# The first load of an attention block, issued as two halves of 64 rows from two engines

## The chip, the cores and the metric

The kernel runs on one core of a Trainium2 chip. A core has TensorE (PE, matmuls), VectorE (DVE), ScalarE (ACT), GpSimd (POOL) and SyncE (SP), and 16 DMA engines that carry the transfers. SyncE and ScalarE can each issue transfers, each into a queue of its own; on chip memory has 128 rows (partitions). The metric is the time of one execution in microseconds (us). Before the change the median of three runs is 1300.84 us (1300.77 to 1301.26).

## The reference

One decoding step of a transformer block, two tokens in the batch, 32 heads, 8192 cached keys and values for each, all in 32 bit floats:

```python
B, Sq, D = 2, 1, 512
H, Sk, Dh = 32, 8192, 128
q = (x @ wq).reshape(B, Sq, H, Dh)          # x is layer-normalised first
scores = einsum("bhqd,bhkd->bhqk", q, k_cache) * (Dh ** -0.5)
p = softmax(scores)
o = einsum("bhqk,bhkd->bhqd", p, v_cache)
h = x + o @ wo
out = h + relu(layernorm(h) @ w1 + b1) ** 2 @ w2 + b2   # F = 1792
```

Keys and values are 64 pairs (batch, head) of 8 MB each, 512 MB in all; the weights wq and wo are 8 MB each.

## The kernel before

On-chip memory holds a ring of three places, each 128 rows of 64 KB (`ring`, `place(u)`). The host has laid out the keys and values of each pair as such a block of 128 rows (`kvd[i]`, keys in the first half of each row, values in the second) and the query weights in the same form (`wqd`), so that each load is one transfer of 128 rows.

Start: place 2 is loaded with the query weights (line 213), issued by SyncE, then x is loaded twice into two rows of `xr` (line 216, after a memset of `xr` on VectorE), then the first two pairs go into places 0 and 1 (line 218). VectorE and ScalarE normalise x, TensorE turns it (`xn`) and multiplies it with the query weights in place 2 (64 matmuls), turns the result, and VectorE writes the queries `QT`, `q3` and `QR`. Once the query matmuls are done, SyncE issues the load of pair 2 into place 2 (line 307).

Loop: 21 rounds of three pairs. For each pair TensorE makes the scores (line 345), VectorE their negated maximum (351), ScalarE the exponentials (358), VectorE the four sums weighted with the values (363) and a copy of the statistics (367), which frees the place. SyncE waits for that and issues the next load into the place (329). The last pair, `wo`, `w1` and `w2` follow by the same queue in pieces, and the feed-forward part runs at the end.

What sets the order: the program is written out by hand. Outside the loop it goes through the class `Line`. `Line.load(out, in_, engine="sp")` records one transfer that the named engine issues (line 136), with a semaphore of its own; `plan` works out from the regions which earlier operations each one waits for, and lets SyncE have at most `AHEAD` = 8 of these loads under way. Loads issued by another engine are not counted there. Operations keep their order on each engine. The operations that read all of place 2 wait for every load that wrote to it.

Of the kernel before, what the change touches and what calls it, by code (L numbers as in the profile page):

```python
# [10 lines left out]
P = 128  # L11
# [162 lines left out]
def attention_block_kernel(nc, xd, kvd, wqd, wod, w1d, w2d, out):  # L174
    def sb(name, *shape):
        return nc.alloc_sbuf_tensor(name, [P, *shape], F32).ap()

    written = nc.alloc_semaphore("written")
    line = Line(nc)
    pe, dve, act, sp = nc.tensor, nc.vector, nc.scalar, nc.sync  # L180
# [11 lines left out]
    def place(u):  # L192
        return ring[:, u * ROW : (u + 1) * ROW]
# [16 lines left out]


    xr = sb("xr", D)
    line.load(place(2), wqd)
    line.memset(xr, 0.0)
    for at in (0, 32):
        line.load(xr[at : at + B], xd)
# [406 lines left out]
```

## Time and profile before

| | us |
|---|---|
| median of three runs | 1300.84 |
| the profiled execution | 1301.16 |
| its span | 1299.8 |
| VectorE busy | 742.9 |
| TensorE busy | 422.4 |
| ScalarE busy | 143.7 |

The profile is of one execution. A line of the timeline gives start and duration in us, the engine and the line of the program, the operation, what it writes and reads, and in brackets how long the engine was idle before it and what ended that. "SPq" is the issue of a transfer by SyncE. "DMA" in a page is the busy share of the 16 DMA engines in tenths in each of 40 equal slices of the span, "GB/s" what they moved in each. A row of DMA issues ends with the median us from the issue to the landing. In a row by stretches the last two columns are the DMA share and the rate.

### The profile page before, as it was taken

Reading aid. Unit: us, or ns where it says so; the run is one execution under the profiler, and the core shown is the slowest. Engines: PE = TensorE matmul, PEld = TensorE weight load, DVE = VectorE, ACT = ScalarE, POOL = GpSimd, SP = SyncE. Lnnn points to the kernel's source line nnn. Section 1 sums busy time; section 2 is a strip of 40 time slices with the busy share of each in tenths; the row PEclk is TensorE's granted clock in tenths of the full one; section 3 lists DMA queues with packets and bytes.
Section 4 is the critical chain, followed back from the end, with each engine's and each line's share of the span. In section 5 each row is a group of like instructions: output and inputs, shape, how many; then the busy total and the mean of one; then the engine's idle time right before and its main releaser. Section 6 shows DMA issues by size and latency. Waiting matters only on the chain. (4 is left out here: it accounts for less than half of the span.)

```text
span 1299.8 us, 6711 instructions
## 1 busy us (share of the span) xinstructions
PE 422.4 (32%) x2418; PEld 113.7 (9%) x2418; DVE 742.9 (57%) x709; ACT 143.7 (11%) x149; POOL 0.7 (0%) x6
## 2 busy tenths in 40 slices
PE   1423233223323323313313323322323332331347
PEld 0100000000000000000000000000000000000012
DVE  1355655655665564665665565665566565657474
ACT  1110010111011011011011011011101011101111
POOL 0000000000000000000000000000000000000000
PEclk9766566666566566656566556656656656666678
DMA  9999999999999999999999999999999999999998
GB/s 420 420 450 419 450 421 442 430 426 446 422 448 421 450 422 442 430 430 442 422 450 421 448 424 448 422 450 421 436 436 421 450 422 448 424 448 422 450 412 371
DMA packets 11069, 561.16 MB, mean 432 GB/s; under 512 B 1234, under 2 KB 1332, under 8 KB 1720
## 3 DMA queue, kind: packets, MB, share of 16 engines
q1 hardware_dynamic: 11064, 561.08, 99.7%
q8 instruction: 4, 0.07, 0.0%
q14 instruction: 1, 0.01, 0.0%
HBM read 561.03 MB, written 0.05 MB: 432 GB/s over the span
## 5 line engine op out<-in xcount | busy, mean ns | idle before, releaser
L345 PE MATMUL s<-ring,q 128*32 128x512 f32 x2016 | 376.1, 914 | 831.2 <-PEq L318 831.2
L363 DVE SCALAR_TENSOR_TENSOR ring<-ring,s 128x2048 f32<-128x2048 f32 x252 | 561.5, 2285 | 143.1 <-DVEq L318 143.1
L351 DVE TENSOR_REDUCE st<-s 128x1 f32<-128x2048 f32 x63 | 144.4, 2292 | 341.9 <-DVEq L318 341.9
L358 ACT ACTIVATE s<-s,st 128x2048 f32<-128x2048 f32 x63 | 122.3, 1942 | 1083.4 <-ACTq L318 1083.4
L345 PEld LDWEIGHTS s<-ring,q 128*32 128x32 f32 x2016 | 94.5, 159 | 1112.0 <-issue 1112.0
L363 DVE DVE_READ_ACCUMULATOR ring<-ring,s 128x1 f32 x252 | 21.0, 83 | 0.0
L367 DVE TENSOR_SCALAR ALL<-st 128x6 f32 x63 | 10.8, 172 | 15.2 <-DVEq L318 15.2
L165 DVE TENSOR_REDUCE sx<-xr 2x1 f32<-2x512 f32 x1 | 0.7, 676 | 21.2 <-DMA xr<-in_xd 21.2
L358 ACT ACTIVATION_READ_ACCUMULATOR s<-s,st 128x1 f32 x63 | 12.1, 193 | 0.0
L139 PE MATMUL s<-ring,OT 128*2 128x512 f32 (+1 forms) x70 | 10.8, 689 | 3.6 <-DMA ring<-in_wod 3.0
L139 PE MATMUL s<-ident,xr 128*128 128x4 f32 x8 | 1.9, 356 | 26.0 <-DVE xr L157 26.0
L139 PE MATMUL s<-ring,xn 128*2 128x512 f32 x64 | 9.2, 742 | 0.3 <-DVE xn L150 0.3
L161 DVE SCALAR_TENSOR_TENSOR ring<-ring,s 128x2048 f32<-128x2048 f32 x3 | 6.8, 2283 | 1.4 <-DMA ring<-in_kvd 1.4
L139 PE MATMUL s<-ring,QR 128*32 128x512 f32 x32 | 5.3, 825 | 4.6 <-DMA ring<-in_kvd 4.6
L157 DVE TENSOR_SCALAR QT<-s 128x64 f32<-128x64 f32 x1 | 0.2, 225 | 10.3 <-PE s L139 10.3
L139 PE MATMUL s<-ring,xc 128*2 128x448 f32 (+1 forms) x34 | 5.6, 725 | 0.3 <-DVE xc L153 0.3
L143 ACT ACT_TABLE_LOAD x4 | 5.1, 1283 | 0.8 <-PEq L615 0.7
L354 DVE TENSOR_SCALAR q<-QT 128x96 f32 x21 | 5.1, 243 | 0.0
L139 PE MATMUL s<-ALL,pick 128*128 128x62 f32 (+1 forms) x16 | 3.4, 352 | 5.1 <-PEq L464 4.5
L139 PE MATMUL s<-ring,a 128*2 128x128 f32 x112 | 3.6, 272 | 2.5 <-DMA ring<-in_w2d 1.8
L139 PEld LDWEIGHTS s<-ident,xr 128*128 128x128 f32 x8 | 1.8, 327 | 26.0 <-DVE xr L157 26.0
L150 DVE COPY res<-s 128x128 f32<-128x128 f32 x1 | 0.3, 292 | 5.9 <-PE s L139 5.9
(86 smaller groups left out, 50.9 us busy)
## 6 DMA issues: line engine op xcount, KB each, us to landing
ring<-in_kvd SPq DMA_DIRECT2D x1, 4096.0 KB, 28.3
ring<-in_wod SPq DMA_DIRECT2D x1, 4096.0 KB, 18.1
ring<-in_kvd SPq DMA_DIRECT2D x1, 3584.0 KB, 26.3
ring<-in_w1d SPq DMA_DIRECT2D x2, 1792.0 KB, 24.8
ring<-in_wod SPq DMA_DIRECT2D x1, 2560.0 KB, 31.8
ring<-in_w2d SPq DMA_DIRECT2D x2, 1280.0 KB, 30.5
ring<-in_wod SPq DMA_DIRECT2D x1, 1568.0 KB, 18.2
ring<-in_kvd SPq DMA_DIRECT2D x63, 37.3
```

The lines of the kernel that those rows point to most:

```text
L139: self.op("pe", lambda e: e.matmul(out, lhsT, rhs, start=start, stop=stop), [lhsT, rhs], [out])
L143: self.op("act", lambda e: e.activation(out, in_, func, bias=bias, scale=scale, accum_out=accum_out), [in_, *more], [out] + ([] if accum_o ...
L150: self.op("dve", lambda e: e.tensor_copy(out, in_), [in_], [out])
L157: self.op("dve", lambda e: e.tensor_scalar(out, in_, by, None, op0=ALU.mult), [in_, *more], [out])
L161: self.op("dve", lambda e: e.scalar_tensor_tensor(out, a, by, b, op0=op0, op1=op1, accum_out=accum_out), [a, b, *more], [out] + ([] if acc ...
L165: self.op("dve", lambda e: e.tensor_reduce(out, in_, axis=AX.X, op=op, negate=negate), [in_], [out])
L345: made = pe.matmul(bk[n][32 * j : 32 * j + 32, :], q3[:, u, :], keys(u)[:, j, n * BLK : (n + 1) * BLK], start=True, stop=True)
L351: dve.tensor_reduce(nm, s, axis=AX.X, op=ALU.max, negate=True).then_inc(m_full, 1)
L354: dve.tensor_scalar(q3, nxt[:, :, None].to_broadcast([P, SLOTS, 32]), 1.0, None, op0=ALU.mult)
L358: act.activation(s, s, AF.Exp, bias=nm, scale=1.0, accum_out=ls).then_inc(e_full, 1)
L363: made = dve.scalar_tensor_tensor(v, v, 1.0, s, op0=ALU.mult, op1=ALU.mult, accum_out=st3[:, u, 2 + e : 3 + e])
L367: dve.tensor_scalar(all3[:, bass.ds(r, 1), u], st3[:, u : u + 1], 1.0, None, op0=ALU.mult).then_inc(kv_free, 1)
```

## The change

The load of the query weights into place 2 is issued as two loads of 64 rows. Rows 0 to 63 stay with SyncE, as its first issue. Rows 64 to 127 are issued by ScalarE, and as nothing stands before that in its program, this is ScalarE's first instruction, ahead of its first table load. The query matmuls wait for both.

```diff
     xr = sb("xr", D)
-    line.load(place(2), wqd)
+    line.load(place(2)[: P // 2], wqd[: P // 2])
+    line.load(place(2)[P // 2 :], wqd[P // 2 :], "act")
     line.memset(xr, 0.0)
     for at in (0, 32):
         line.load(xr[at : at + B], xd)
```

All lines behind it have numbers higher by one. No other load is changed.

## The prediction

> **What bounds the kernel now.** I read the page first: the span, the busy shares, the rate of the transfers in 40 slices and the chain that ended last.
>
> ```profile
> span 1299.8 us, 6711 instructions
> PE 422.4 (32%) x2418; PEld 113.7 (9%) x2418; DVE 742.9 (57%) x709; ACT 143.7 (11%) x149; POOL 0.7 (0%) x6
> DMA  9999999999999999999999999999999999999998
> GB/s 420 420 450 419 450 421 442 430 426 446 422 448 421 450 422 442 430 430 442 422 450 421 448 424 448 422 450 421 436 436 421 450 422 448 424 448 422 450 412 371
> DMA packets 11069, 561.16 MB, mean 432 GB/s; under 512 B 1234, under 2 KB 1332, under 8 KB 1720
> q1 hardware_dynamic: 11064, 561.08, 99.7%
> DMA ring<-in_w2d 2%; DMA ring<-in_kvd 2%; PE s L139 0%; SPq L136 0%; DVE res L150 0%; SPq L469 0%
> ```
>
> The busiest compute engine, VectorE, works for 57% of the span, while the transfers on the one queue q1 fill 99.7% of what 16 DMA engines could do in it. The chain ends in transfers too: each of its large pieces is a load. So bytes over rate set the time. The second view, busy time by stretches, gives that rate where nothing disturbs it:
>
> ```profile
> core 0: us, PE busy (x) PEld busy (x) DVE busy (x) ACT busy (x) POOL busy (x), PEclk, DMA share, GB/s
> 60.00:1200.00 1140.00, 354.22 (x1888) 88.62 (x1888) 673.88 (x611) 121.46 (x118) 0.00 (x0) 0.61 1.00 434
> 1183.00:1222.00 39.00, 10.42 (x64) 2.75 (x64) 23.78 (x22) 4.12 (x4) 0.00 (x0) 0.68 1.00 432
> 2.00:41.00 39.00, 12.96 (x88) 5.35 (x88) 4.34 (x16) 5.39 (x9) 0.00 (x0) 1.00 0.96 415
> ```
>
> From 60 to 1200 us the DMA engines are busy all the time (share 1.00) and move 434 GB/s. A full load is 128 rows of 64 KB, 8.39 MB, eight rows for each of 16 engines: 8.39 MB / 434 GB/s = 19.33 us, and one row on one engine 19.33 / 8 = 2.42 us. The program moves 561.16 MB; at 434 GB/s that is 1293.0 us of the 1299.8. All but some 7 us of the span is this one stream, and nothing behind it can win back time that it loses.
>
> The third view is the loads from issue to landing:
>
> ```profile
> ring<-in_wqd SPq DMA_DIRECT2D x1, 22.0
> ring<-in_kvd SPq DMA_DIRECT2D x63, 37.3
> ```
>
> The first load, the one that is split, lands 22.0 us after its issue: 19.33 of transfer and 2.7 of start and completion. A key/value load takes 37.3, so it stands 37.3 - 19.3 = 18.0 us in a queue that is still full. That reserve is why the stream never runs dry in the loop.
>
> **The change, part by part.** The order of work around the first load is in the timeline:
>
> ```profile
> start us, us, engine line op out<-in xcount [idle before <-releaser]
> 0.74 1.28 ACT L143 ACT_TABLE_LOAD   x1 [0.74 <-PEq L615]
> 0.75 0.40 SPq L136 DMA_DIRECT2D ring<-in_wqd  x1
> 0.92 0.48 DVE L147 MEMSET xr<- 128x512 f32 x1 [0.92 <-PEq L615]
> 1.43 0.62 SPq L136 DMA_DIRECT2D xr<-in_xd  x2
> 2.03 1.12 ACT L143 ACTIVATE s<-zero 128x512 f32<-128x512 f32 x2
> 2.09 0.91 SPq L218 DMA_DIRECT2D ring<-in_kvd  x2
> 3.15 1.28 ACT L143 ACT_TABLE_LOAD   x1
> 22.80 0.68 DVE L165 TENSOR_REDUCE sx<-xr 2x1 f32<-2x512 f32 x1 [21.24 <-DMA xr<-in_xd]
> 24.95 0.29 ACT L143 ACTIVATE sx<-sx,eps_t 2x1 f32<-2x1 f32 x1 [20.51 <-DVE xs L161]
> 28.19 9.21 PE L139 MATMUL s<-ring,xn 128*2 128x512 f32 x64 [0.33 <-DVE xn L150]
> 37.48 0.33 SPq L307 DMA_DIRECT2D ring<-in_kvd  x1
> 42.22 5.34 PE L345 MATMUL s<-ring,q 128*32 128x512 f32 x32 [2.94 <-PEq L318]
> 62.02 0.34 SPq L329 DMA_DIRECT2D ring<-in_kvd  x1
> ```
>
> *Issue on SyncE.* The issue stays first there and covers half the rows, so it takes between 0.2 and 0.4 us instead of 0.40. The two loads of x behind it wait for the memset of xr, which ends at 0.92 + 0.48 = 1.40, so they and the two key/value loads stay where they are. Worth 0; with the start of the stream itself, at most 0.2 us gained.
>
> *Issue on ScalarE.* One issue of 0.2 to 0.4 us goes ahead of its first table load at 0.74. The two clears and the second table load end at 4.43 now, at about 4.8 then; ScalarE is next wanted at 24.95, after 20.51 us of idle time. Cost 0. Without that cover it would be 0.4.
>
> *One more wait.* The first query matmul now waits for two loads instead of one. It starts at 28.19, long after the landing at 22.8, since it waits for xn too. Cost 0. One more load also brings one completion for each DMA engine; 16 small packets beside 1234 cost nothing that shows.
>
> *The order of bytes.* SyncE's queue now holds half of the first load, x, then the key/value loads. ScalarE's queue holds the other half. Bytes ahead of x and of the loads behind are the same if both queues are served alike. Where ScalarE's half falls behind, the queries come later: they release the reload of place 2, issued at 37.48. The stream has work until about 2 + 3 x 19.33 = 60 us, so 22 us of lateness are hidden there.
>
> *The rate of the two halves.* This is the one cost that can be large, and no row of this trace shows it: every load that reaches 434 GB/s has 128 rows, and each DMA engine carries its eight of them. Afterwards each engine carries four rows of the lower 64 and four of the upper 64. If what limits an engine is the engine itself, the halves cost 0. If it is the place to which it writes, 16 engines on 64 rows share half of those places, a row takes 2 x 2.42 us, and the first 8.39 MB take 38.7 us: +19.33. What decides whether alternation between the halves helps is whether the engines are in step. A close view of the rate, in 40 slices of 1.05 us from 0 to 42 us, shows that they are:
>
> ```profile
> GB/s 0 687 312 0 811 187 62 936 0 999 0 874 125 250 749 0 999 0 936 62 380 626 0 999 0 999 0 749 250 62 936 0 999 0 874 125 250 749 0 999
> ```
>
> Bytes are booked at one end of a row here. In two or three slices, one row's time of 2.42 us, all of an interval's 999 GB/s falls into one slice or two neighbours: the 16 engines change rows together. So if they alternate between the queues row by row, they are all in the lower half, then all in the upper, and the halves do not complement each other. An engine that is ahead of its partner saves its lead on every row. The lead is at most one slice, 1.05 us, which leaves 8 x (2 x 2.42 - 1.05) = 30.3 us, +11.0; with no lead it is +19.33. Most slices are 999 beside 0 or 936 beside 62, so the lead is nearer to nothing: I take 0.2 us, 8 x (4.84 - 0.2) = 37.1, or +17.8.
>
> The ends are thus 0 (below it by the 0.2 of the issue; 434 GB/s is reached already in all the other loads, so a faster stream is excluded) and +19.33; were start and completion, 2.7 us, paid a second time because the halves follow each other, +22.0. I take +17.8, because the only rate of this trace belongs to 128 rows at once, and because the engines in step speak against a free ride. All of it reaches the end: the stream is the bound and has no hole later to absorb it.
>
> [...]
>
> *Sum.* The profiled execution took 1301.16 us, 1.4 outside its span of 1299.8. 1301.16 + 0 + 0 + 0 + 17.8 = 1319.0. The median of the runs shown is 1300.84, 0.3 below, so the forecast is 1318.6.
>
> **The rivals.** *No change.* The limit is each DMA engine, or the engines mix both queues so finely that both halves are written all the time. For it: the first load runs at almost the steady rate (415 GB/s from 2 to 41 us, start-up included), every load ends at the same 434, and all issue costs are covered. Against it: no load of fewer rows at that rate, and the engines in step. Time: 1300.84 - 0.2 to + 0.4, about 1300.8. It decides as soon as a 64-row half runs at more than 0.88 of 434 GB/s (19.33 / 0.88 = 22.0, +2.6). [...]
>
> *Half way.* Pairs of engines drift apart so that one writes low while its partner writes high: +2.6 to +11.0, about 1308. For it: leads of 62 to 250 GB/s worth in some slices. Against it: a lead does not grow where two share evenly, since the one ahead waits as long as the other.
>
> *The second queue does not run beside the first.* If ScalarE's half starts late, SyncE's half goes first on its own, and ScalarE's shares the engines with the first key/value load. With a limit by place that still costs 11 to 19 us; with a limit by engine, nothing, for the 22 us of cover above. It adds no time of its own.
>
> *Faster.* A gain over 2.6 us would need nearly all of the first load's 2.7 us of start and completion to vanish; only the 0.40 of issue is touched.
>
> **How the numbers follow.** Over 0.2% (2.6 us) is about what a measurement of this kernel can tell from no change. Chances: half rate 0.62, half way 0.08, no change 0.28, faster 0.02. So slower 0.70, same 0.28, faster 0.02. The likeliest case's own range is +11.0 to +22.0: 1311.8 to 1322.9. Leaving out "no change" would leave out more than 2 in 10, so the range goes down to it: 1300.4 to 1323.
>
> **What would show it.** Right: the first slice of the rate row falls from 420 to 250 GB/s or less and the second slice is low in part; the halves land near 38 to 40 us after issue instead of 22.0; VectorE's wait for x grows from 21.2 to 35 to 40; everything from the first loop matmul (42.22) on is 17 to 19 us later at an unchanged 434. ScalarE's first table load starts near 1.1 us, with no wait behind it. A second hardware queue of 4.2 MB appears. Wrong: the first slice stays at 420 and the landings near 22, or the first slices are slow and the end is not later, in which case the stream had a reserve that I do not see.

## The result and the profile after

The median of six executions rose from 1300.86 to 1320.84 us: 20.0 us more, a ratio of 1.0152 with a 95% interval of 1.014 to 1.0163. One of the six executions after took 1477.41 us and one of five of the first experiment's kernel below 1512.89 us, both for reasons that are not known, and the ratios are of the others alone. The profiled execution has a span of 1319.5 us.

The page after, busy shares, rate in 40 slices (33 us each now), packets and queues:

```profile
span 1319.5 us, 6712 instructions
PE 419.8 (32%) x2418; PEld 113.4 (9%) x2418; DVE 742.8 (56%) x709; ACT 143.6 (11%) x149; POOL 0.7 (0%) x6
GB/s 223 352 442 443 417 443 443 417 443 441 419 443 441 419 443 441 419 443 441 419 443 441 419 443 439 421 443 435 425 443 431 429 443 425 435 443 423 435 429 372
DMA packets 11085, 561.16 MB, mean 425 GB/s; under 512 B 1250, under 2 KB 1348, under 8 KB 1736
q1 hardware_dynamic: 11000, 556.89, 98.2%
q10 hardware_dynamic: 80, 4.19, 1.5%
```

The bytes are the same and so is the work of the engines. The loss stands in the first slice and a part of the second: 223 instead of 420 GB/s, then the old rate to the end. The new queue q10 is ScalarE's, with half of the query weights, 4.19 MB. Its 80 packets are 64 rows of 64 KB and 16 of 4 bytes, and the total of packets rose by 16 for the one load more. A half is carried by all 16 engines: where each half runs alone, in the first experiment below, their busy share is 1.01 and 1.07.

The issue rows of the two halves, with the time from issue to landing at the end, and the stretches of the rate (columns as before, DMA share and GB/s last):

```profile
ring<-in_wqd SPq DMA_DIRECT2D x1, 42.3
ring<-in_wqd ACTq DMA_DIRECT2D x1, 42.1
ring<-in_kvd SPq DMA_DIRECT2D x63, 37.3
```

```profile
2.00:41.00 39.00, 0.00 (x0) 0.00 (x0) 0.00 (x0) 3.01 (x4) 0.00 (x0) 1.00 1.02 218
60.00:1200.00 1140.00, 351.31 (x1888) 88.37 (x1888) 670.86 (x607) 121.42 (x118) 0.00 (x0) 0.62 1.00 434
```

Both halves land together, 42.3 and 42.1 us after their issue instead of 22.0. Up to 41 us the stream moves 218 GB/s while the DMA engines count as busy all the time (share 1.02): they are not short of work, each row takes longer. A row's time and bytes are booked whole, so the figures of a short stretch are rough and a share can pass 1.00. The packet records of the trace are sharper: in the change each row after the first on an engine took about 4.90 us, against 2.42 us before. Afterwards it is 434 GB/s again and the later loads take 37.3 us to landing, as before. The timeline shows the shift passed on whole:

```profile
0.74 0.57 SPq L136 DMA_DIRECT2D ring<-in_wqd  x1
0.74 0.55 ACTq L136 DMA_DIRECT2D ring<-in_wqd  x1
1.32 1.28 ACT L143 ACT_TABLE_LOAD   x1 [1.32 <-PEq L616]
1.44 0.95 SPq L136 DMA_DIRECT2D xr<-in_xd  x2
2.42 0.93 SPq L219 DMA_DIRECT2D ring<-in_kvd  x2
3.74 1.28 ACT L143 ACT_TABLE_LOAD   x1
43.51 0.68 DVE L165 TENSOR_REDUCE sx<-xr 2x1 f32<-2x512 f32 x1 [41.95 <-DMA xr<-in_xd]
48.90 8.78 PE L139 MATMUL s<-ring,xn 128*2 128x512 f32 x64 [0.33 <-DVE xn L150]
57.75 0.33 SPq L308 DMA_DIRECT2D ring<-in_kvd  x1
62.42 5.34 PE L346 MATMUL s<-ring,q 128*32 128x512 f32 x32 [2.85 <-PEq L319]
82.22 0.36 SPq L330 DMA_DIRECT2D ring<-in_kvd  x1
```

The first matmul of the loop starts at 62.42 instead of 42.22, and the first reload inside the loop is issued at 82.22 instead of 62.02: 20.2 us later, both. The span is 19.7 longer, so next to nothing is won back.

### The profile page after: what moved, and what is told of

It is laid out like the page before. It is cut to its first block, busy times and chain, and to the rows that moved or that the text cites. A ratio compares the mean times of both kernels' runs of the same rounds, so it can differ in the third digit from the quotient of the medians.

```text
span 1319.5 us, 6712 instructions
## 1 busy us (share of the span) xinstructions
PE 419.8 (32%) x2418; PEld 113.4 (9%) x2418; DVE 742.8 (56%) x709; ACT 143.6 (11%) x149; POOL 0.7 (0%) x6
## 3 DMA queue, kind: packets, MB, share of 16 engines
q10 hardware_dynamic: 80, 4.19, 1.5%
## 5 line engine op out<-in xcount | busy, mean ns | idle before, releaser
L139 PE MATMUL s<-ring,OT 128*2 128x512 f32 (+1 forms) x70 | 11.8, 792 | 2.5 <-DMA ring<-in_wod 1.9
## 6 DMA issues: line engine op xcount, KB each, us to landing
ring<-in_kvd SPq DMA_DIRECT2D x63, 37.3
```

The costliest lines, as they stand in the source:

```text
L139: self.op("pe", lambda e: e.matmul(out, lhsT, rhs, start=start, stop=stop), [lhsT, rhs], [out])
```

## The experiments

Three explanations were set against each other: *place* (the rows that are written limit the rate), *alternation* (an engine that serves two queues is slow) and *shape* (any transfer of 64 rows is slow). All kernels differ from the kernel before in the lines shown, and each is compared with runs of the kernel before on the same chip.

### Both halves from one queue

```diff
-    line.load(place(2), wqd)
+    line.load(place(2)[: P // 2], wqd[: P // 2])
+    line.load(place(2)[P // 2 :], wqd[P // 2 :])
```

> Both halves of 64 rows are issued by SyncE, one after the other; ScalarE issues nothing. If the cost lies in where the 16 DMA engines write (place), the lower half goes first at half rate and the upper half after it, 8 rows for each engine at about 4.9 us: 19 to 20 us slower than before, like the change. If the cost lies in the engines' alternation between two queues (alternation), it is gone: within 0.5 us of before. If any transfer of 64 rows is slow whatever its rows (shape), 19 to 20 us slower.

Measured: 1322.05 us against 1300.96, ratio 1.0168 (1.0151 to 1.0185). The second queue is not the cause: without it the loss is as large, even 1.1 us larger than in the change (21.1 against 20.0). The kernel was run once more for its profile.

> Both halves of 64 rows by SyncE, as in one_queue, for a profile. Place: 21 us slower as before, each row 4.9 us; the lower half done near 22 us, the upper near 42 us, x behind both.

Measured: 1322.17 against 1301.12, ratio 1.0171 (1.0154 to 1.0188). The rate by stretches of this kernel:

```profile
2.00:22.00 20.00, 0.00 (x0) 0.00 (x0) 0.00 (x0) 2.43 (x4) 0.00 (x0) 1.00 1.01 210
22.00:41.00 19.00, 0.00 (x0) 0.00 (x0) 0.00 (x0) 0.00 (x0) 0.00 (x0) 1.00 1.07 221
60.00:1200.00 1140.00, 351.85 (x1894) 88.59 (x1893) 670.26 (x606) 121.48 (x118) 0.00 (x0) 0.62 1.00 435
```

The lower half runs at 210 and the upper, alone, at 221 GB/s: about half of 434 for each. By the packet records a row took about 5.1 us in either half.

### Two queues, halves by columns

```diff
-    line.load(place(2), wqd)
+    line.load(place(2)[:, :HALF], wqd[:, :HALF])
+    line.load(place(2)[:, HALF:], wqd[:, HALF:], "act")
```

> Two halves again, one by SyncE and one by ScalarE, but each of all 128 rows and half of the columns, so rows of 32 KB. Place: each engine writes its own rows all the time, within 0.5 us of before. Alternation: 19 to 20 us slower, as the engines alternate between two queues just as in the change. Shape: within 0.5 us of before.

Measured: 1301.04 against 1300.96, ratio 1.0 (0.9991 to 1.001). Two queues served at once cost 0.1 us here, which is nothing that shows; alternation falls. The issue rows and the first stretch:

```profile
ring<-in_wqd ACTq DMA_DIRECT2D x1, 4096.0 KB, 21.9
ring<-in_wqd SPq DMA_DIRECT2D x1, 4096.0 KB, 22.1
```

```profile
2.00:41.00 39.00, 12.99 (x88) 5.35 (x88) 4.33 (x16) 5.82 (x9) 0.00 (x0) 1.00 0.98 422
```

The two halves share the rate of one whole load (422 GB/s, against 415 before) and land when it did, 21.9 and 22.1 us after their issue against 22.0.

### Other 64 rows

```diff
-    line.load(place(2), wqd)
+    line.load(place(2)[32:96], wqd[32:96])
+    line.load(place(2)[:32], wqd[:32])
+    line.load(place(2)[96:], wqd[96:])
```

> Three loads by SyncE alone: rows 32 to 95 (64 rows), then 0 to 31, then 96 to 127. Place, with rows 0 to 63 on one half of the write places and 64 to 127 on the other: the middle 64 rows reach both halves and run at full rate, 4 rows for each engine at 2.42 us, 9.7 us; the two outer loads have 2 rows for each engine at 4.9 us each, 9.8 us apiece; 29.2 us in place of 19.3, so 9.9 us slower. Shape: the middle 64 rows take 19.6 us and the outer ones 9.8 each or more, 19.9 us slower or more. Alternation: within 0.5 us of before.

Measured: 1311.64 against 1300.96, ratio 1.0088 (1.0071 to 1.0105): 10.7 us slower where place gave 9.9 and shape at least 19.9. Its stretches, cut where the middle rows should end:

```profile
2.00:12.00 10.00, 0.00 (x0) 0.00 (x0) 0.00 (x0) 2.42 (x4) 0.00 (x0) 1.00 1.03 419
12.00:31.00 19.00, 0.00 (x0) 0.00 (x0) 0.00 (x0) 0.00 (x0) 0.00 (x0) 1.00 1.04 221
```

Rows 32 to 95 run at 419 GB/s, start included. Rows 0 to 31 and 96 to 127 run at 221. So a transfer of 64 rows is not slow as such (419 GB/s here, 210 and 221 from the one queue above); it matters which rows, and 32 rows of one half run at about the rate of its 64 (221).

### The whole load from ScalarE

```diff
-    line.load(place(2), wqd)
+    line.load(place(2), wqd, "act")
```

> The first load whole, 128 rows, issued by ScalarE; SyncE's queue begins with x and the first key/value load, which then share the engines with it row by row. Place and shape: all rows at 2.42 us, within 0.5 us of before; the query weights land near 41 us instead of 22, and the reload of place 2 is issued near 57 us, still hidden because the stream has work until about 60 us. Alternation: 16 rows of each engine at 4.9 us, up to 40 us slower.

Measured: 1300.92 against 1300.96, ratio 0.9999 (0.999 to 1.0009). Its issue row and two lines of its timeline:

```profile
ring<-in_wqd ACTq DMA_DIRECT2D x1, 39.0
```

```profile
2.13 0.91 SPq L218 DMA_DIRECT2D ring<-in_kvd  x2
48.89 0.33 SPq L307 DMA_DIRECT2D ring<-in_kvd  x1
```

ScalarE's queue is as fast as SyncE's here: 409 GB/s from 2 to 41 us against 415 before, and the same time at the end. The weights shared the engines with the first key/value load, landed 17 us later than before (39.0 us after the issue against 22.0), and the reload of place 2 went out at 48.89 instead of 37.48: 11.4 us late, and free, since the stream still had work. Here 11.4 us of lateness inside the cover cost nothing; the rate lost in the change cost 20.0 us. The expected 57 us for the reload was too late, because it left out that x and its normalisation came early here: the query matmuls could start as soon as the weights had landed.

### Every other row

```diff
-    line.load(place(2), wqd)
+    line.load(place(2)[::2], wqd[::2])
+    line.load(place(2)[1::2], wqd[1::2], "act")
```

> Two loads of 64 rows, one by SyncE and one by ScalarE, but SyncE takes rows 0, 2, 4 ... and ScalarE rows 1, 3, 5 ... . If what counts is which rows a transfer reaches altogether, both loads reach all write places: within 0.5 us of before. If what counts is where the 16 engines write at one moment, it depends on which rows they hold in step: between 0 and 20 us slower. [...]

Measured: 1301.25 against 1301.12, ratio 1.0001 (0.9992 to 1.0011). A close view of the rate (40 slices, 0 to 42 us), first of the change, then of this kernel:

```profile
GB/s 0 125 874 0 0 0 687 312 0 0 62 874 62 0 0 187 811 0 0 0 749 250 0 0 62 874 62 0 0 187 811 0 0 0 811 187 0 0 62 878
```

```profile
GB/s 0 125 874 0 250 749 0 999 0 936 62 437 562 0 999 0 999 0 687 312 2 1005 0 999 0 811 187 125 874 0 999 0 936 62 437 562 0 999 0 936
```

In both the 16 engines change rows in step, with groups of slices that sum to about 999 GB/s over 1.05 us, one row of 64 KB for each of 16 engines. In the change they come nearly five slices apart, here little more than two. The packet records show in both kernels that the engines take turns between the queues: 16 rows of ScalarE's load, then 16 of SyncE's, and so on. Two sets of 64 rows from two queues, in step, at the full rate (419 GB/s from 2 to 22 us): being in step is not enough to lose, and the loads that lost (218 GB/s in the change, 221 for the outer rows above) each had all their rows in one half of the memory. Of the 0 to 20 us expected for the case that what counts is where the engines write at one moment, 0.1 came; which engine holds which row, no run here shows.

### Written or read

In all kernels so far the rows that are read from the weights moved together with the rows that are written. Two kernels take them apart:

```diff
-    line.load(place(2), wqd)
+    line.load(place(2)[: P // 2], wqd[::2])
+    line.load(place(2)[P // 2 :], wqd[1::2], "act")
```

> The two sides of the transfer taken apart. Written as in the change: rows 0 to 63 by SyncE, 64 to 127 by ScalarE. Read as in every_other: even rows of the weights for the one, odd rows for the other (the weights thus stand in permuted rows, so the queries are other numbers; the work is the same). If the price lies in the rows that are written, 20 us slower; if it lies in the rows that are read, within 0.5 us of before.

```diff
-    line.load(place(2), wqd)
+    line.load(place(2)[::2], wqd[: P // 2])
+    line.load(place(2)[1::2], wqd[P // 2 :], "act")
```

> The reverse: written as in every_other (even rows by SyncE, odd rows by ScalarE), read as in the change (the first 64 rows of the weights for the one, the last 64 for the other; permuted weights again). If the price lies in the rows that are written, within 0.5 us of before; if in the rows that are read, 20 us slower.

Measured: 1320.87 and 1301.31 against 1300.94, ratios 1.0152 (1.0135 to 1.0169) and 1.0003 (0.9993 to 1.0012). Their issue rows, of the first and of the second:

```profile
ring<-in_wqd ACTq DMA_DIRECT2D x1, 42.3
ring<-in_wqd SPq DMA_DIRECT2D x1, 42.5
```

```profile
ring<-in_wqd SPq DMA_DIRECT2D x1, 22.4
ring<-in_wqd ACTq DMA_DIRECT2D x1, 22.2
```

The price goes with the rows that are written: 19.9 us, against the 20.0 of the change. With the rows that are read goes 0.4 us at most.

### Half the dose, and a dose at the end

```diff
-    line.load(place(2), wqd)
+    line.load(place(2)[: P // 2, :HALF], wqd[: P // 2, :HALF])
+    line.load(place(2)[P // 2 :, :HALF], wqd[P // 2 :, :HALF], "act")
+    line.load(place(2)[:, HALF:], wqd[:, HALF:])
```

> Only the first half of the columns (32 KB of each row) is loaded in two halves of 64 rows by SyncE and ScalarE; the second half of the columns follows as one load of 128 rows. If the price is the bytes moved at half rate: 4.19 MB at 434 GB/s is 9.7 us, so 9.7 to 10 us slower. If it were a price for each split load or for the start alone, 19 to 20 us slower again, or near 0.

Measured: 1310.36 against 1301.12, ratio 1.0072 (1.0055 to 1.0089): 9.2 us, a little under half of the 20.0 and under the 9.7 expected. Its first stretches:

```profile
2.00:22.00 20.00, 0.00 (x0) 0.00 (x0) 0.00 (x0) 3.02 (x4) 0.00 (x0) 1.00 1.03 236
22.00:41.00 19.00, 5.38 (x28) 2.48 (x32) 3.77 (x13) 1.78 (x3) 0.00 (x0) 1.00 1.01 435
```

The rate is low while the two halves are carried and whole again behind them. The halves have as many rows as in the change, each half as long, and the price is halved: it is one of bytes.

```diff
     def load_half(i, half):
         cut = slice(half * HALF, (half + 1) * HALF)
-        line.load(slot(i)[:, cut], kvd[i][:, cut])
+        line.load(slot(i)[: P // 2, cut], kvd[i][: P // 2, cut])
+        line.load(slot(i)[P // 2 :, cut], kvd[i][P // 2 :, cut])
```

> The first load is whole, as before. The keys of the last pair (128 rows of 32 KB, issued 77 us before the end) are loaded in two halves of 64 rows, both by SyncE. If the stream has no reserve anywhere, 4.19 MB at half rate costs 9.7 to 10 us at the end too; if the loads and sums behind it can absorb lateness, less.

Measured: 1312.96 against 1301.12, ratio 1.0092 (1.0075 to 1.0109): 11.8 us. The stretches in which those keys are carried:

```profile
1240.00:1250.00 10.00, 6.53 (x32) 1.57 (x32) 1.38 (x4) 0.00 (x0) 0.00 (x0) 0.58 1.01 210
1250.00:1260.00 10.00, 0.00 (x0) 0.00 (x0) 7.84 (x7) 2.06 (x2) 0.00 (x0) 0.59 0.95 206
```

At about 208 GB/s the 4.19 MB take 20.2 us in place of 9.7, which is 10.5 of the 11.8. The stream has no reserve there either. The other 1.3 us are not explained. One more of SyncE's loads counts towards its limit of eight, and the issues of the four pieces of `w2` took 22.28 us in all, with their waits, against 13.07 before; whether that is the cause is not shown.

## Why the prediction was right

*The bound.* The stream at 434 GB/s sets the time, and what it loses at the start is not won back. Right: the same 434 from 60 to 1200 us, the loop is 20.2 us later, and the late dose costs no less for its bytes (11.8 us for 4.19 MB).

*Issue on SyncE and ScalarE.* Forecast: 0.2 to 0.4 us for each, no move of the loads behind. Measured: 0.57 and 0.55, longer than the 0.40 of the whole load; the key/value loads were issued at 2.42 instead of 2.09, and ScalarE's table load at 1.32, not 1.1. The cost is still 0 under its cover: ScalarE's second table load ends at 3.74 + 1.28 = 5.02, and it is then idle until 45.66.

```profile
45.66 0.29 ACT L143 ACTIVATE sx<-sx,eps_t 2x1 f32<-2x1 f32 x1 [40.63 <-DVE xs L161]
```

*One more wait, and the order of bytes.* Right: the first query matmul still starts as soon as xn is there (48.90, idle 0.33 on VectorE), and the reload at 57.75 came in time for a stream that, by an estimate from the measured 39 and 19.3 us, then had work until about 2 + 39 + 2 x 19.3 = 80 us.

*The rate of the two halves.* The right end was taken. It was chosen between ends of 0 and +19.33 with the trace silent; the runs now show the rates: 210 to 221 GB/s for rows of one half of the memory, from one queue or from two, and 419 for 64 rows that lie across both, rows 32 to 95 from one queue or alternate rows from two. What in the memory or in the engines sets them, no run shows. The choice was a judgement all the same: no load of 64 rows stood in the trace before, and the range reached down to no change, so that the time lies inside it says little. The term was mis-sized: +17.8 forecast, 20.0 measured. The step that failed is the lead of 0.2 us that an engine was to save on each row, my estimate; no run shows such a saving. From the landing, (42.2 - 2.7) / 8 = 4.94 us a row, and 4.90 by the packet records, not 4.64, and not less than twice 2.42. The price was a little more than half the rate in this kernel (2.42 / 4.90 = 0.49 of it was left), and a row took 6% longer than assumed.

*In step.* That the engines change rows together was read rightly, and they do so in the change as well, with the queues in turn, 16 rows of the one and 16 of the other, as the prediction had it. As a sign against a free ride it was too weak: alternate rows kept the step and cost nothing that shows (1301.25 us against 1301.12). Whether halves would be free if the engines were out of step was not tried.

*The rivals.* No change (0.28) was refuted by the slices and landings; the range's lower end, 1300.4, is 0.2 below what its terms add up to. Half way (+2.6 to +11.0) did not come about. ScalarE's half did not start late: both issues stand at 0.74. The signs listed for the forecast appeared, some beyond their marks: 223 in the first slice, landings at 42 (a little past the 38 to 40), VectorE's wait for x at 41.95 (past the 35 to 40), the loop 20.2 us later (past the 17 to 19). Those three lie 1 to 2 us beyond their marks, and the whole is 2.2 us beyond the forecast.

## What to carry to other kernels

In a kernel bound by its transfers, cut a load by columns or by alternate rows, not into rows 0 to 63 and 64 to 127: such halves ran at 210 to 221 GB/s here, from one queue or from two, against 434, while columns ran at 422 and alternate rows at 419, start included. A second issuing engine cost no rate here, and where the rows ran at the full rate it brought none (1301.04 us by columns against 1300.96). Before hoping that a loss at the start is absorbed, look whether the stream has holes later: with a busy share of 1.00 from 60 to 1200 us, nearly all of the 20.2 us lost here reached the end, while lateness behind a full queue (11.4 us of it with the whole load from ScalarE) was free (1300.92 us against 1300.96).

## What was not expected of the hardware

- The issue of 64 rows took 0.57 us on SyncE in the change, that of 128 rows 0.40 before. That both engines issue at once is not the reason: the halves by columns, 128 rows each, took 0.40 and 0.39 us so, and SyncE alone took 1.20 us for two loads of 64 rows, and 1.19 with the dose at the end.
- Halves from one queue cost more than from two: 21.1 us, twice, against 20.0 in the change and 19.9 with the source rows permuted, for the same 8.39 MB. The packet records show the same: against a row of a whole load, a row of a half took up to 2.12 times as long from one queue (5.13 us, and 2.57 where rows are 32 KB) and 1.97 to 2.05 times from two (4.90 and 4.96; 2.39 at half the dose). What makes the difference is open, and the intervals of the ratios overlap.
- Alternate rows cost 0.1 us (1301.25 against 1301.12) even with all engines in step. Which engine carries which row of a stepped transfer stays open.
